# Two heads to a tile in a decode-attention kernel: 48-KB rows, one V buffer, FFN transposed, projection weights last

## The chip, the cores and the metric

The kernel runs on one core of a Trainium2 chip. The metric is the device time of one execution in microseconds (us). Several executions of one kernel agree within about 0.5% here, except single stragglers. Ratios are computed as the mean time of one kernel's fast runs over the mean of the other's fast runs in the same rounds, so they are not quite the ratio of the medians that are quoted.

Engines: DVE is the vector engine, PE the tensor engine (matmuls), ACT the scalar engine, SP the engine that here only issues DMA transfers (copies between HBM, where the inputs lie, and SBUF, the on-chip memory whose 128 partitions hold the tiles), in the order of the program. PV is short for the matmuls of the probabilities with V.

## The reference, cut to what matters

One decode step for four batches: layernorm, then attention over the last 2,048 positions of a cache of 8,192, for 32 heads of width 192, plus a SwiGLU feed-forward net (FFN), both added to x. All in bf16.

```python
W = min(4096, max(256, Sk // 4))                  # 2048
k = k_cache[:, :, Sk - W:, :]; v = v_cache[:, :, Sk - W:, :]   # [4, 32, 2048, 192]
scores = einsum("bhqd,bhkd->bhqk", q, k) * Dh ** -0.5
o = einsum("bhqk,bhkd->bhqd", softmax(scores), v)
out = x + o.reshape(B, 1, 6144) @ wo + (silu(xn @ w1) * (xn @ w3)) @ w2
```

Each byte of K and V is used once. 4 x 32 x 2,048 x 192 elements of 2 bytes, twice, are 201 of the 223 MB that are loaded.

## The kernel before

A tile of K or V is one head, for all four batches. Partition q = 4 p + b holds 64 neighbouring positions of batch b, so a row is 64 x 192 x 2 = 24,576 bytes (24 KB). The source of the transfer is *named* as 32 x 4 rows: 32 values of p outermost, then the 4 batches.

```python
def load_k(h):
    kt = kpool.tile([P, NJ, Dh], BF16, tag="kt")          # 2 buffers; V has 3
    nc.sync.dma_start(out=kt[:].rearrange("q j d -> q (j d)"),
                      in_=k_win[:, h].rearrange("b (p j) d -> p b (j d)", p=PB))   # 32 x 4 x 12288
...
def mult(u):      # DVE: a quarter of K times q, broadcast over positions
def adder(u):     # PE: six 128x512 matmuls with the identity add up 32-wide pieces
def reduce_quarter(u)   # DVE: the last sum over 32
def pv(h, half):  # PE: probabilities times V, two positions per matmul
def ge_tr(h):     # PE: float32 matmuls that regroup o for the projection with wo
```

A head is four slots (u) of this; softmax steps of earlier heads are scheduled between them. At the end come wo for the last heads and w2, whose 24 matmuls are the last work.

Of the kernel before, what the change touches and what calls it, by code (L numbers as in the profile page):

```python
# [18 lines left out]
def kernel(  # L19
# [14 lines left out]
    KBUFS: int = 2,  # L34
    VBUFS: int = 3,
    PBUFS: int = 4,
    L: int = 10,
    FFN_HEAD: int = 6,
# [9 lines left out]
    PB = P // B  # L48
    NJ = W // PB
    GQ = 4  # L50
    JQ = NJ // GQ
    NK = Dh // DD
    SCALE = float(Dh) ** -0.5
# [5 lines left out]
    NU = H * GQ  # L59
    N0 = D // 2  # L60
    N1 = D - N0
    QC = 512
    NQ = H * Dh // QC
    assert D % P == 0 and F % QC == 0 and P % B == 0 and W % (PB * GQ) == 0
    assert JQ * DD == 512 and JQ % 2 == 0 and 2 * Dh <= 512 and 0 < N1 <= 512
    assert (H * Dh) % QC == 0 and NQ % 6 == 0 and QW % P == 0 and Dh % RPP == 0 and P == HG * CT
    assert 2 * H * Dh <= NJ * Dh and KBUFS == 2 and VBUFS == 3 and L == 10

# [3 lines left out]
    kpool = ctx.enter_context(tc.tile_pool(name="kt", bufs=KBUFS))  # L72
    vpool = ctx.enter_context(tc.tile_pool(name="vt", bufs=VBUFS))
    ppool = ctx.enter_context(tc.tile_pool(name="pr", bufs=PBUFS))
    wopool = ctx.enter_context(tc.tile_pool(name="wo", bufs=2))
    small = ctx.enter_context(tc.tile_pool(name="small", bufs=3))
# [4 lines left out]
    ps_acc = ctx.enter_context(tc.tile_pool(name="ps_acc", bufs=1, space=MemoryType.PSUM))  # L81


    k_win = A_k_cache[:, :, Sk - W:Sk, :]
    v_win = A_v_cache[:, :, Sk - W:Sk, :]
    kts, vts, prs, pss, scs, exs, zs = {}, {}, {}, {}, {}, {}, {}
    wos, o_raws, rsums, rtbs, chs, ges, oTs = {}, {}, {}, {}, {}, {}, {}

    def load_k(h):
        kt = kpool.tile([P, NJ, Dh], BF16, tag="kt")  # L90
        nc.sync.dma_start(out=kt[:].rearrange("q j d -> q (j d)"),
                          in_=k_win[:, h].rearrange("b (p j) d -> p b (j d)", p=PB))
        kts[h] = kt

    def load_v(h, pieces=1):
        vt = vpool.tile([P, NJ, Dh], BF16, tag="vt")
        src = v_win[:, h].rearrange("b (p j) d -> p b j d", p=PB)
        n = NJ // pieces
        for i in range(pieces):
            nc.sync.dma_start(out=vt[:, i * n:(i + 1) * n, :].rearrange("q j d -> q (j d)"),  # L100
                              in_=src[:, :, i * n:(i + 1) * n, :].rearrange("p b j d -> p b (j d)"))
        vts[h] = vt

    def wo_load(hg):
        wo_t = wopool.tile([P, RPP * D], BF16, tag="wo")
        nc.sync.dma_start(out=wo_t[:], in_=A_wo[hg * QW:(hg + 1) * QW, :].rearrange("(p i) n -> p (i n)", i=RPP))
        wos[hg] = wo_t

    x_sb = const.tile([B, D], BF16, name="x_sb")
    nc.sync.dma_start(out=x_sb[:], in_=A_x.rearrange("b s d -> (b s) d"))  # L110
    wq_v = A_wq.rearrange("(p kc) n -> p kc n", kc=KC)
    wq_rows = []
    for k0 in range(0, KC, 2):
        n = min(2, KC - k0)
        wt = vpool.tile([P, 2, H * Dh], BF16, tag="vt")
        nc.sync.dma_start(out=wt[:, 0:n, :].rearrange("p k n -> p (k n)"),
                          in_=wq_v[:, k0:k0 + n, :].rearrange("p k n -> p (k n)"))
        wq_rows += [wt[:, i, :] for i in range(n)]
    for h in range(KBUFS):
        load_k(h)  # L120
# [5 lines left out]
    ones_ff = const.tile([P, P], FP32, name="ones_ff")  # L126
    nc.vector.memset(ones_ff[:], 1.0)

    mask_f = const.tile([P, B], FP32, name="mask_f")
    nc.vector.tensor_reduce(out=mask_f[:], in_=idf[:].rearrange("q (p b) -> q b p", b=B), axis=AX.X, op=ALU.add)  # L130
    mask_b = const.tile([P, B], BF16, name="mask_b")
    nc.vector.tensor_copy(out=mask_b[:], in_=mask_f[:])

    sel = const.tile([P, 2 * B], FP32, name="sel")
    nc.vector.tensor_reduce(out=sel[:], in_=idf[:].rearrange("q (c k) -> q k c", k=CT)[:, 0:2 * B, :],
                            axis=AX.X, op=ALU.add)

# [6 lines left out]
    xc = ppool.tile([B, D], FP32, tag="pr")  # L144
    nc.vector.tensor_scalar_add(out=xc[:], in0=xf[:], scalar1=negmean[:, 0:1])
    sq = ppool.tile([B, D], FP32, tag="pr")
    ssq = const.tile([B, 1], FP32, name="ssq")
    nc.scalar.activation(out=sq[:], in_=xc[:], func=ACTF.Square, accum_out=ssq[:])
# [6 lines left out]
    xn = const.tile([B, D], BF16, name="xn")  # L155
    nc.vector.tensor_scalar_mul(out=xn[:], in0=xc[:], scalar1=rstd[:, 0:1])
# [5 lines left out]
    xnT = const.tile([P, KC, PB, B], BF16, name="xnT")  # L162
    nc.vector.tensor_copy(out=xnT[:], in_=xnT_ps[:].unsqueeze(2).to_broadcast([P, KC, PB, B]))


    qbc = const.tile([P, H * Dh], BF16, name="qbc")
    for c0 in range(0, NQ, 6):
        qps = [pool.tile([P, QC], FP32, tag=tag, name="qps")
               for pool, tag in ((ps_add, "ps"), (ps_add, "ps"), (ps_o, "o_ps"), (ps_o, "o_ps"), (ps_m, "mt"), (ps_t, "t"))]
        for kc in range(KC):  # L170
            for i, qp in enumerate(qps):
                nc.tensor.matmul(qp[:], lhsT=xnT[:, kc].rearrange("p a b -> p (a b)"),  # L172
                                 rhs=wq_rows[kc][:, (c0 + i) * QC:(c0 + i + 1) * QC],
                                 start=(kc == 0), stop=(kc == KC - 1))
        for i, qp in enumerate(qps):
            dst = qbc[:, (c0 + i) * QC:(c0 + i + 1) * QC]
            if i % 2:
                nc.vector.tensor_copy(out=dst, in_=qp[:])  # L178
            else:
                nc.scalar.copy(out=dst, in_=qp[:])  # L180
# [8 lines left out]
    acc0 = ps_acc.tile([B, N0], FP32, name="acc0")  # L189
    acc1 = ps_acc.tile([B, N1], FP32, name="acc1")  # L190
# [8 lines left out]
    def mult(u):  # L199
        h, g = u // GQ, u % GQ  # L200
        pr = ppool.tile([P, JQ, Dh], BF16, tag="pr")
        nc.vector.tensor_tensor(out=pr[:], in0=kts[h][:, g * JQ:(g + 1) * JQ, :],  # L202
                                in1=qbc[:, h * Dh:(h + 1) * Dh].unsqueeze(1).to_broadcast([P, JQ, Dh]),
                                op=ALU.mult)
        prs[u] = pr
        if g == GQ - 1:
            kts.pop(h)
# [9 lines left out]
    def reduce_quarter(u):  # L217
        h, g = u // GQ, u % GQ
        if g == 0:
            scs[h] = small.tile([P, NJ], FP32, tag="sc", name="sc")  # L220
        nc.vector.tensor_reduce(out=scs[h][:, g * JQ:(g + 1) * JQ], in_=pss.pop(u)[:], axis=AX.X, op=ALU.add)  # L221

    def chain_lmax(h):
        lmax = small.tile([P, 1], FP32, tag="lmax")
        nc.vector.tensor_reduce(out=lmax[:], in_=scs[h][:], axis=AX.X, op=ALU.max)
        chs[h] = [lmax]

    def chain_tr(h):
        mt = ps_m.tile([P, P + 1 + B], FP32, tag="mt")
        nc.tensor.transpose(out=mt[0:1, 0:P], in_=chs[h][0][:], identity=idf[:])  # L230
        chs[h].append(mt)

    def chain_gmax(h):
        gmax = small.tile([1, B], FP32, tag="gmax")
        nc.vector.tensor_reduce(out=gmax[:], in_=chs[h][1][0:1, 0:P].rearrange("o (p b) -> o b p", b=B),  # L235
                                axis=AX.X, op=ALU.max)
        gneg = small.tile([1, PB, B], FP32, tag="gneg")
        nc.vector.tensor_scalar_mul(out=gneg[:], in0=gmax[:].unsqueeze(1).to_broadcast([1, PB, B]), scalar1=-SCALE)
        chs[h].append(gneg)

    def chain_bc(h):
        lmax, mt, gneg = chs[h]
        nc.tensor.matmul(mt[:, P:P + 1], lhsT=gneg[:].rearrange("o p b -> o (p b)"), rhs=ones_ff[0:1, 0:1],  # L243
                         start=True, stop=True)
        negm = small.tile([P, 1], FP32, tag="negm")
        nc.scalar.copy(out=negm[:], in_=mt[:, P:P + 1])
        rsum = small.tile([P, 1], FP32, tag="rsum", bufs=4)
        ex = small.tile([P, NJ], BF16, tag="ex")
        nc.scalar.activation(out=ex[:], in_=scs.pop(h)[:], func=ACTF.Exp, bias=negm[:, 0:1], scale=SCALE,  # L249
                             accum_out=rsum[:])  # L250
        rsums[h] = rsum
        exs[h] = ex

    def chain_z(h):
        ex = exs.pop(h)
        z = small.tile([P, NJ, B], BF16, tag="z")
        nc.vector.tensor_tensor(out=z[:], in0=ex[:].unsqueeze(2).to_broadcast([P, NJ, B]),  # L257
                                in1=mask_b[:].unsqueeze(1).to_broadcast([P, NJ, B]), op=ALU.mult)
        zs[h] = z

    def pv(h, half):
        o_ps, z, vt = o_banks[h % 2], zs[h], vts[h]
        n = NJ // 4
        for jj in range(half * n, (half + 1) * n):
            c = jj % 4
            nc.tensor.matmul(o_ps[c * CT:c * CT + 2 * B, :], lhsT=z[:, 2 * jj:2 * jj + 2, :],  # L266
# [31 lines left out]
    def ge_copy(h):  # L298
        hg, hl = h // HG, h % HG
        sl = slice(hl * CT, (hl + 1) * CT)  # L300
        if hl == 0:
            oTs[hg] = small.tile([P, RPP, B], BF16, tag="oT", bufs=2, name="oT")
# [132 lines left out]
```

## Time and profile before

| | before |
|---|---|
| median, 3 runs | 533.06 us (532.88 to 534.96) |
| loaded | 223 MB, 419 GB/s over the span |
| share of the span in which the load queue is busy | 97.8% |
| DVE, PE busy | 66%, 73% |

Lines of the page of the kernel before: engine totals, then the rate of the DMA in 40 slices of 13.3 us, the packets, and the load queue (packets, MB, share of 16 engines' span).

```profile
span 533.2 us, 6724 instructions
PE 391.0 (73%) x2949; PEld 177.6 (33%) x2949; DVE 349.4 (66%) x471; ACT 48.2 (9%) x150; POOL 1.1 (0%) x8
GB/s 353 430 428 431 421 442 424 438 435 428 425 435 432 428 433 431 431 427 439 429 428 431 435 426 438 430 428 435 430 433 428 433 428 440 435 420 372 422 390 140
DMA packets 11709, 223.39 MB, mean 419 GB/s; under 512 B 1304, under 2 KB 1312, under 8 KB 2720
q1 hardware_dynamic: 11680, 222.97, 97.8%
```

The queue hardly rests, and its rate is flat for most of the span. The table of windows of the kernel before (stretch, length, busy time of PE, PEld, DVE, ACT and POOL with their instructions, share of its full clock that PE was granted, share of DMA, GB/s) says the same closer, and shows the two largest places where loads were missing: a dip at 482 to 487 us, and the end. A packet counts in the window in which it starts, so a short window can show a share above 1.

```profile
100.00:200.00 100.00, 75.11 (x576) 33.97 (x576) 66.23 (x88) 13.62 (x34) 0.00 (x0) 0.88 1.00 430
200.00:300.00 100.00, 73.05 (x581) 33.47 (x581) 69.97 (x94) 5.99 (x24) 0.00 (x0) 0.83 1.01 432
482.00:487.00 5.00, 4.89 (x31) 1.55 (x29) 3.91 (x7) 0.00 (x0) 0.00 (x0) 0.82 0.57 238
524.50:533.20 8.70, 5.82 (x31) 2.91 (x28) 0.48 (x1) 0.41 (x1) 0.00 (x0) 0.80 0.02 10
```

The waits of the kernel before (engine and line, what it waited for: us in total, times, longest) show DVE waiting for K:

```profile
DVE pr L202 <- DMA kt<-in_A_k_cache_dram: 99.2, 29, 7.9
```

So the kernel is bound by its loads; 518 of its 533 us are 223.4 MB at 431 GB/s.

### The profile page before, as it was taken

The page shows a single profiled execution, that of the slowest core. Times are in us where ns is not written, and L with a number is a line of the kernel's source. Part 1 is how long each engine was busy: PE and PEld are TensorE (multiplying, and loading weights), DVE is VectorE, ACT ScalarE, POOL GpSimd, SP SyncE. Part 2 cuts the span into 40 slices and gives each one's busy share as a digit, 9 for nine tenths or more (in the row PEclk, how much of TensorE's full clock was granted, in tenths as well). Part 3 has the DMA queues.
Part 4 walks back from the last instruction along what each step waited for, and adds up shares of the span by engine and source line. Part 5 has one row for each costly group of instructions (what it writes and reads, how often), then busy time and mean ns, then how long its engine had stood idle before and what let it go on. Part 6 is the DMA issues. An engine that isn't in the chain of part 4 may idle for free.

```text
span 533.2 us, 6724 instructions
## 1 busy us (share of the span) xinstructions
PE 391.0 (73%) x2949; PEld 177.6 (33%) x2949; DVE 349.4 (66%) x471; ACT 48.2 (9%) x150; POOL 1.1 (0%) x8
## 2 busy tenths in 40 slices
PE   2876776867686978676947688586749868587987
PEld 0322232333142433232413334233313324232544
DVE  3177775787384776776757777578657778477860
ACT  2111000000222000000000000000000000000010
POOL 0000000000000000000000000000000000000000
PEclk9879776899698797688989969689996769777998
DMA  8999999999999999999999999999999999998993
GB/s 353 430 428 431 421 442 424 438 435 428 425 435 432 428 433 431 431 427 439 429 428 431 435 426 438 430 428 435 430 433 428 433 428 440 435 420 372 422 390 140
DMA packets 11709, 223.39 MB, mean 419 GB/s; under 512 B 1304, under 2 KB 1312, under 8 KB 2720
## 3 DMA queue, kind: packets, MB, share of 16 engines
q1 hardware_dynamic: 11680, 222.97, 97.8%
q8 instruction: 23, 0.38, 0.3%
q14 instruction: 6, 0.05, 0.0%
HBM read 222.96 MB, written 0.01 MB: 418 GB/s over the span
## 4 chain that ended last, share of the span: by engine, by line
DMA 59%; DVE 22%; PE 17%; issue 1%; ACT 0%; SPq 0%
DMA kt<-in_A_k_cache_dram 56%; DVE pr L202 17%; PE ps L213 7%; PE gp L294 5%; DVE sc L221 4%; DMA wt<-in_A_wq_dram 3%; PE qps L172 2%; PE o_ps L266 1%; PE acc_239 L194 1%; PE acc_240 L195 1%; DVE oT L303 1%; DVE rtb L284 1%; DVE qbc L178 0%; ACT o_raw L272 0%; DVE o_ps L186 0%
## 5 line engine op out<-in xcount | busy, mean ns | idle before, releaser
L213 PE MATMUL ps<-pr,idb 128*128 128x512 bf16 x768 | 228.9, 445 | 119.8 <-DVE sc L221 116.3
L202 DVE TENSOR_TENSOR pr<-kt,qbc 128x3072 bf16<-128x3072 bf16 x128 | 223.9, 1750 | 100.2 <-DMA kt<-in_A_k_cache_dram 99.2
L213 PEld LDWEIGHTS <-idb 128*128 128x128 bf16 x768 | 79.5, 108 | 219.8 <-issue 166.7
L221 DVE TENSOR_REDUCE sc<-ps 128x16 f32<-128x512 f32 x128 | 87.5, 684 | 10.1 <-PE ps L213 9.1
L266 PE MATMUL o_ps<-vt,z 128*8 128x384 bf16 x1024 | 59.3, 356 | 0.0
L294 PEld LDWEIGHTS gp<-sel,o_raw 128*32 128x32 f32 x768 | 46.8, 151 | 21.3 <-issue 19.2
L272 ACT COPY o_raw<-o_ps 128x384 f32<-128x384 f32 x32 | 15.3, 479 | 405.4 <-PE o_ps L266 405.4
L294 PE MATMUL gp<-sel,o_raw 128*32 128x4 f32 x768 | 49.6, 199 | 1.1 <-ACT o_raw L272 0.6
L266 PEld LDWEIGHTS <-z 128*8 128x8 bf16 x1024 | 21.1, 89 | 41.6 <-issue 32.6
L284 DVE RECIPROCAL rtb<-mt 32x4 f32<-32x4 f32 x32 | 5.7, 179 | 32.2 <-PE gp L294 31.9
L172 PE MATMUL qps<-wt,xnT 128*128 128x512 bf16 x60 | 17.7, 463 | 4.9 <-DMA wt<-in_A_wq_dram 4.9
L178 DVE CAST qbc<-qps 128x512 bf16<-128x512 f32 x6 | 3.8, 684 | 19.4 <-PE qps L172 19.4
L257 DVE TENSOR_TENSOR z<-ex,mask_b 128x256 bf16<-128x256 bf16 x32 | 13.2, 414 | 2.4 <-ACT ex L249 2.4
L194 PE MATMUL acc_239<-wo_t,oT 128*4 128x320 bf16 x48 | 13.8, 305 | 0.3 <-DVE oT L303 0.3
L195 PE MATMUL acc_240<-wo_t,oT 128*4 128x320 bf16 x48 | 13.8, 306 | 0.0
L243 PEld LDWEIGHTS mt<-ones_ff,gneg 1*128 1x128 f32 x64 | 9.4, 182 | 10.2 <-issue 9.6
L243 PE MATMUL mt<-ones_ff,gneg 1*128 1x1 f32 x64 | 12.1, 256 | 0.0
L172 PEld LDWEIGHTS <-xnT 128*128 128x128 bf16 x60 | 6.9, 115 | 15.3 <-issue 10.2
L249 ACT ACTIVATE ex<-sc,negm 128x64 bf16<-128x64 f32 x32 | 11.1, 348 | 1.0
L326 PE MATMUL gt<-w_756,xnT 128*4 128x512 bf16 x15 | 6.9, 622 | 4.2 <-DVE oT L303 2.9
L230 PE MATMUL mt<-idf,lmax 128*1 128x128 f32 x32 | 9.2, 287 | 0.0
L235 DVE TENSOR_REDUCE gmax<-mt 1x4 f32<-1x128 f32 x32 | 8.6, 269 | 0.7 <-PE mt L230 0.7
(59 smaller groups left out, 98.4 us busy)
## 6 DMA issues: line engine op xcount, KB each, us to landing
kt<-in_A_k_cache_dram SPq DMA_DIRECT2D x32, 3072.0 KB, 20.5
vt<-in_A_v_cache_dram SPq DMA_DIRECT2D x31, 3072.0 KB, 25.7
wo_t<-in_A_wo_dram SPq DMA_DIRECT2D x8, 960.0 KB, 19.4
wt<-in_A_wq_dram SPq DMA_DIRECT2D x2, 3072.0 KB, 9.8
vt<-in_A_v_cache_dram SPq DMA_DIRECT2D x2, 1536.0 KB, 14.1
w_756<-in_B_w_dram SPq DMA_DIRECT2D x1, 1920.0 KB, 23.4
w_1001<-in_B_w_dram SPq DMA_DIRECT2D x1, 1920.0 KB
wt<-in_A_wq_dram SPq DMA_DIRECT2D x1, 1536.0 KB, 19.8
```

Source lines behind the costliest of these rows:

```text
L172: nc.tensor.matmul(qp[:], lhsT=xnT[:, kc].rearrange("p a b -> p (a b)"), rhs=wq_rows[kc][:, (c0 + i) * QC:(c0 + i + 1) * QC], start=(kc == ...
L194: nc.tensor.matmul(acc0[:], lhsT=lhsT, rhs=rhs[:, 0:N0], start=first, stop=last)
L195: nc.tensor.matmul(acc1[:], lhsT=lhsT, rhs=rhs[:, N0:D], start=first, stop=last)
L202: nc.vector.tensor_tensor(out=pr[:], in0=kts[h][:, g * JQ:(g + 1) * JQ, :], in1=qbc[:, h * Dh:(h + 1) * Dh].unsqueeze(1).to_broadcast([P, ...
L213: nc.tensor.matmul(ps[:], lhsT=idb[:], rhs=pr[:, :, kk * DD:(kk + 1) * DD], start=(kk == 0), stop=(kk == NK - 1))
L221: nc.vector.tensor_reduce(out=scs[h][:, g * JQ:(g + 1) * JQ], in_=pss.pop(u)[:], axis=AX.X, op=ALU.add)
L243: nc.tensor.matmul(mt[:, P:P + 1], lhsT=gneg[:].rearrange("o p b -> o (p b)"), rhs=ones_ff[0:1, 0:1], start=True, stop=True)
L249: nc.scalar.activation(out=ex[:], in_=scs.pop(h)[:], func=ACTF.Exp, bias=negm[:, 0:1], scale=SCALE, accum_out=rsum[:])
L257: nc.vector.tensor_tensor(out=z[:], in0=ex[:].unsqueeze(2).to_broadcast([P, NJ, B]), in1=mask_b[:].unsqueeze(1).to_broadcast([P, NJ, B]), ...
L266: nc.tensor.matmul(o_ps[c * CT:c * CT + 2 * B, :], lhsT=z[:, 2 * jj:2 * jj + 2, :], rhs=vt[:, 2 * jj:2 * jj + 2, :], start=(jj < 4), stop= ...
L272: nc.scalar.copy(out=o_raw[:].rearrange("q two d -> q (two d)"), in_=o_ps[:])
L294: nc.tensor.matmul(gp[sl, i, :], lhsT=o_raw[:, part, i:Dh:RPP], rhs=sel[:, part * B:(part + 1) * B], start=(part == 0), stop=(part == 1))
```

## The change

Its intent is larger transfers and fewer small instructions. Heads i and i+16 share a tile: partition q = 8 p + u, u = (batch, head of the pair), holds 128 positions, so rows have 48 KB and a tile 6 MB. V has one buffer; K runs one pair ahead of V; w2 and the last two wo tiles are issued after the last V. The FFN's products are made transposed. The core of the diff:

```diff
-    GQ = 4
+    U = 2 * B
+    PU = P // U                      # 16
+    NJ = W // PU                     # 128
+    GQ = 8
-    vpool = ctx.enter_context(tc.tile_pool(name="vt", bufs=VBUFS))
+    vpool = ctx.enter_context(tc.tile_pool(name="vt", bufs=1))
-    k_win = A_k_cache[:, :, Sk - W:Sk, :]
+    k_win = A_k_cache[:, :, Sk - W:Sk, :].rearrange("b (h i) s d -> i (b h) s d", h=2)
+    def load_pair(dst, win, i, j0, j1):
+        src = win[i].rearrange("u (p j) d -> p u j d", p=PU)
+        nc.sync.dma_start(out=dst[:, j0:j1, :].rearrange("q j d -> q (j d)"),
+                          in_=src[:, :, j0:j1, :].rearrange("p u j d -> p u (j d)"))   # 16 x 8 x 24576
... (softmax chain and masks for 8 units; regrouping in 6 matmuls a pair instead of 12 a head; FFN transposed)
+        if i >= 2:
+            add(u0 - GQ, 0, load_k, i)
+        if not final:
+            add(u0 + 1, 0, load_v, i)
+        v = ul + 7 if not final else ul + 6       # PV of pair i: slots 6 and 7 of pair i+1
+        add(v, 7, pv, i, 0, NJ // 2 if not final else VCUT[1])
...
+    add(NU, 0, load_v, NP - 1, VCUT)
+    add(NU, 0, w2_load, 0)
+    add(NU, 0, wo_load, NG - 2)
+    add(NU, 0, wo_load, NG - 1)
+    for i in range(1, 4):
+        add(NU, 0, w2_load, i)
```

## The prediction

> **What bounds the kernel now.** The DMA queue: the page gives it 97.8% of the 16 engines' span, and the table of windows a flat 430 to 432 GB/s from 100 to 400 us. DVE (66% busy) waits 99 us for K tiles. [...] 223.4 MB at 431 GB/s are 518 us. The other 15 us of the 533.2-us span: 2.1 before the first data; about 4 of dips at 482 to 487 us (a K load issued late) and 505 to 515; 8.7 after the last load (524.5 us), for the last projections and all w2 matmuls.
>
> **What the change does.**
> 1. K and V rows of 48 KB instead of 24. The trace's packet records are linear: median 291 ns for 7,680 B, 573 for 15,360, 912 for 24,576; so 8 ns plus 36.8 per 1,000 B. Estimate for 49,152 B: 1,816 ns, 433 GB/s. 256 packets fewer per engine: -2.3 us with fewer completion packets.
> 2. DVE multiplies, adders and reduces keep shape and number (128 x 1.75 us, 768 x 0.44, 128 x 0.68). The float32 regrouping matmuls fall from 768 (50 us) to 96, softmax chains from 32 to 16. Off the critical path: 0.
> 3. One V slot: V(i) can't be issued until PV(i-1) is done, and PV stands in slots 6 and 7 of pair i, behind seven multiplies of K(i). From K(i) landing: 7 x 1.67 + 6 x 0.6 + 3.5 of chain work on DVE, then adder and two PV halves: about 22.7 us, 24 with issue latency (1.5, read at 485 us). In steady state another K stands behind V(i-1), so the queue is fed until 28 us: 4 us of margin. Estimate: 2 us lost.
> 4. At the end there is no next K. V(14) follows the last K for 14.5 us, then the queue is empty until PV(14) is done. wo and w2 need not wait, but stand behind V(15) in the one in-order SP queue. Estimated gap: 10.4 us without loads.
> 5. wo and w2 last: after the last byte remain four matmuls, the cast and the output: 5 us instead of 8.7. The old dips (4 us) go.
>
> **Sum (all on the critical path).** Start 1.8 + loads 516.3 + early gaps 2 + end gap 10.4 + tail 5 = 535.5 us. The gaps (+12) eat the gains (-10).
>
> Prediction: **535.5 us**, range 528 to 544. Faster by over 2%: 0.04; within 2%: 0.83; slower: 0.13. Without any gap it would be about 523, so a 2% gain is nearly excluded.
>
> **What would show it right or wrong.** (1) K and V packets near 1,816 ns, steady rate near 433. (3) The SP queue's waits: V loads wait for PV, yet the rate holds. (4) A hole of 8 to 12 us without DMA, some 25 us before the loads end, ended by V(15)'s issue after PV(14)'s last matmul. (5) About 5 us from last byte to end, the chain of waits ending in w2's matmuls.
>
> **What would make it wrong.** If DVE or PE are slower per slot than I take (a reduce one slot after its adder waits for PE when the clock is halved), the margin of step 3 goes and every pair opens a gap: 2 us in each of 15 is +30. If 48-KB rows read HBM at another rate, 1% is 5 us.

## The result

The time doubled: median 1047.35 us (1044.82 to 1062.45, 4 runs) against 533.49 us (532.88 to 534.96, 4 runs); ratio of the fast runs 1.9608, 95% interval 1.9545 to 1.9671. The result passed the comparison with the reference, which says little here (see the experiments). One of the four runs after, 1062.45 us, is slow and is not in the ratio.

The same lines of the page, after:

```profile
span 1045.7 us, 5471 instructions
PE 368.8 (35%) x2391; PEld 159.4 (15%) x2391; DVE 358.0 (34%) x428; ACT 26.9 (3%) x78; POOL 1.1 (0%) x8
GB/s 361 211 209 207 209 209 219 209 207 213 239 216 209 202 248 211 219 211 209 211 211 215 209 215 211 207 216 217 211 209 211 211 209 214 209 214 211 120 180 213
DMA packets 7240, 223.32 MB, mean 214 GB/s; under 512 B 808, under 2 KB 816, under 8 KB 2352
q1 hardware_dynamic: 7208, 222.96, 98.0%
```

DVE and PE did about as much work as before (358 and 369 us; 349 and 391 before). The queue is as busy as it was, 98.0%, and moves half as much. That combination is worth a pause: the share of a DMA queue counts packets in flight, not bytes, so a queue that is "98% busy" can be at half rate. Windows and waits of the kernel after:

```profile
400.00:500.00 100.00, 34.68 (x206) 14.17 (x209) 41.87 (x47) 1.73 (x7) 0.00 (x0) 0.69 1.00 212
990.00:998.00 8.00, 7.47 (x76) 2.87 (x75) 0.69 (x1) 0.42 (x1) 0.00 (x0) 0.72 0.00 0
```

```profile
DVE pr L224 <- DMA kt<-in_A_k_cache_dram: 363.4, 16, 26.7
PE o_ps L287 <- DMA vt<-in_A_v_cache_dram: 198.7, 16, 17.5
SPq L91 <- DMA vt<-in_A_v_cache_dram: 795.3, 15, 58.5
```

DVE and PE wait for K and V. The last line is the SP queue waiting for the V tile that lies in the only V buffer; it is no cause of the half rate, as the queue of loads was full all the while (share 0.99 to 1.01 in each 100 us from 100 to 900 us).

The trace also records each packet. Medians in ns, by packet size (count in brackets; not a view of the page):

```
bytes     before         after
 7,680    291 (1152)     467 (1024)     wo, w2
12,288    460  (384)     728  (256)     last wq row; of the last V before also the halves, after the last quarter
15,360    573  (256)     584  (256)     w1, w3
24,576    912 (8320)     912  (256)     K, V and wq before; wq after
49,152      -           3779 (3968)     K and V after   (estimate in the prediction: 1,816)
```

Three things stand in this table. The 48-KB packets take 2.08 times the estimate. The small packets have grown too, but only those that ran beside K or V: the first wo packets of each of six such episodes take some 600 ns, and only in the first episodes do they fall to about 300 on the way; the last two wo tiles, which run after the last V, take 291 to 308 throughout (wo is now named 64 x 2; the kernel before took 291). And the last quarter of the last V comes in packets of 12,288 bytes, which took up to 974 ns, as slow per byte as the 48-KB ones. This points away from the size of a packet; what else it is, the experiments have to show.

### The profile page after: what moved, and what is told of

Read it like the earlier page. It is cut to its first block, busy times and chain, and to the rows that moved or that the text cites. A ratio compares the mean times of both kernels' runs of the same rounds, so it can differ in the third digit from the quotient of the medians.

```text
span 1045.7 us, 5471 instructions
## 1 busy us (share of the span) xinstructions
PE 368.8 (35%) x2391; PEld 159.4 (15%) x2391; DVE 358.0 (34%) x428; ACT 26.9 (3%) x78; POOL 1.1 (0%) x8
## 4 chain that ended last, share of the span: by engine, by line
another core or an unknown queue 51%; PE 20%; DVE 18%; DMA 9%; ACT 1%; issue 0%; SPq 0%; DVEq 0%
DVE pr L224 11%; PE ps L235 11%; DMA vt<-in_A_v_cache_dram 8%; PE o_ps L287 6%; DVE sc L243 3%; DVE z L279 1%; PE qps L194 1%; DMA wq_a<-in_A_wq_dram 1%; PE f_ps L356 1%; DVE o L301 1%; ACT o_odd L293 1%; DVE o_odd L298 1%; PE acc L216 1%; PE acc L217 1%
## 5 line engine op out<-in xcount | busy, mean ns | idle before, releaser
L287 PE MATMUL o_ps<-vt,z 128*16 128x384 bf16 x1024 | 68.1, 427 | 198.7 <-DMA vt<-in_A_v_cache_dram 198.7
L287 PEld LDWEIGHTS <-z 128*16 128x16 bf16 x1024 | 29.5, 107 | 236.2 <-issue 230.4
L279 DVE TENSOR_TENSOR z<-ex,mask_b 128x1024 bf16<-128x1024 bf16 x16 | 19.3, 1209 | 1.2 <-ACT ex L271 1.2
L356 PE MATMUL f_ps<-xnT,w 128*128 128x4 bf16 x120 | 7.8, 199 | 24.4 <-DMA w<-in_B_w_dram 24.4
L325 PE MATMUL gp<-sel,o 128*64 128x4 f32 x192 | 14.6, 205 | 4.9 <-DVE o L301 4.9
L216 PE MATMUL acc<-wo_t,oT 128*4 128x320 bf16 x48 | 15.8, 342 | 0.0
L217 PE MATMUL acc<-wo_t,oT 128*4 128x320 bf16 x48 | 15.5, 339 | 0.0
L325 PEld LDWEIGHTS gp<-sel,o 128*64 128x64 f32 x192 | 13.5, 148 | 12.1 <-PE ps L235 8.7
L194 PE MATMUL qps<-wq_a,xq 128*128 128x384 bf16 x64 | 12.7, 364 | 2.2 <-DMA wq_a<-in_A_wq_dram 2.2
L194 PEld LDWEIGHTS <-xq 128*128 128x128 bf16 x80 | 8.4, 105 | 8.7 <-issue 2.9
L301 DVE TENSOR_TENSOR o<-o_odd,hp 128x384 f32<-128x384 f32 x16 | 8.9, 558 | 0.5
```

The source lines that it names most:

```text
L194: nc.tensor.matmul(qp[:], lhsT=xq[:, h2, kc].rearrange("p a b h -> p (a b h)"), rhs=row[:, h2, c * QC:(c + 1) * QC], start=(kc == 0 and h2 ...
L216: nc.tensor.matmul(acc0[:], lhsT=lhsT, rhs=rhs[:, 0:N0], start=first, stop=last)
L217: nc.tensor.matmul(acc1[:], lhsT=lhsT, rhs=rhs[:, N0:D], start=first, stop=last)
L279: nc.vector.tensor_tensor(out=z[:], in0=ex[:].unsqueeze(2).to_broadcast([P, NJ, U]), in1=mask_b[:].unsqueeze(1).to_broadcast([P, NJ, U]), ...
L287: nc.tensor.matmul(o_ps[c * CT:c * CT + 2 * U, :], lhsT=z[:, 2 * jj:2 * jj + 2, :], rhs=vt[:, 2 * jj:2 * jj + 2, :], start=(jj < 4), stop= ...
L301: nc.vector.tensor_tensor(out=o2[:], in0=o_raw[:].rearrange("q (m r) -> q r m", r=RPP).unsqueeze(3).to_broadcast([P, RPP, CT, 2]), in1=hp[ ...
```

## The experiments

Theories at the start: *size* (a 48-KB row costs more per byte), *addresses* (the rows read together lie at offsets that coincide modulo a power of two), *far heads* (two heads of a batch in one transfer; they are 16 heads of 3 MiB, so 48 MiB, apart, and the 192 MiB in the expectation of e2 is a slip). No view shows which rows are read at one moment. Kernels that move other bytes than the reference asks are wrong. The comparison with the reference passed for all of them, so it is not sharp enough to see which rows of K and V were used. The diffs are cut to the core. A list of pairs of numbers there is an access pattern: step in elements and count of each dimension, from the outermost in; where the kernel has `rearrange`, its line is written here in the same form, so that the two can be compared.

### e1: 48-KB rows as two transfers of 24 KB

```diff
-        load_pair(kts[i], k_win, i, 0, NJ)
+        for j0 in (0, NJ // 2):
+            load_pair(kts[i], k_win, i, j0, j0 + NJ // 2)
```

(V alike.)

> The changed kernel, each row of 48 KB fetched as two transfers of 24 KB (first halves of all rows, then second halves); every byte still lands where it did. Size theory (a row of 48 KB costs twice as much per byte): back to 24-KB packets near 912 ns, about 431 GB/s, 525 to 540 us. Address theory (the rows that the 16 engines read at one moment start at offsets that coincide modulo some power of two, as their pitch of 48 KB and the pairs of heads stay): packets near 1,900 ns, about 213 GB/s, 1,030 to 1,050 us.

Measured: 1031.41 us (before on that chip: 533.07). The 8,320 packets of 24,576 bytes took a median of 1,832 ns, where the same size took 912 before. The size theory has fallen.

### e2: two blocks of 24 KB at a pitch of 24 KB

```diff
+        n = NJ // 2
+        base = (i * Sk + Sk - W + (j0 // n) * PU * n + j0 % n) * Dh
+        src = bass.AP(cache.tensor, base, [[n * Dh, PU], [16 * Sk * Dh, U], [1, (j1 - j0) * Dh]])
```

> As the run before, but a partition takes two blocks of 24 KB that lie 16 blocks apart, so that rows fetched together have a pitch of 24 KB, not 48; K and V are permuted alike, the result stays right. Size theory: the same as the run before. Address theory: if offsets coincide modulo 128 KB, [...] the packets take near 912 ns, 525 to 540 us; if they coincide modulo 64 KB [...] it stays near 1,030 us. Theory of two far heads at once (engines read two heads, 192 MiB apart, at the same moment, and that alone is slow): slow in both runs, near 1,030 us.

Measured: 1014.25 us, 1,828 ns. The pitch does not matter, at least not this one.

### e3: units skewed against each other by 6 KB

```diff
-   [[NJ * Dh, PU], [16 * Sk * Dh, U], [1, n]]
+   [[NJ * Dh, PU], [(16 * Sk - 16) * Dh, U], [1, n]]
```

> The changed kernel with its 48-KB rows and one transfer a tile, but the rows of unit u (batch and head) start 6 KB x u earlier in its head[...]; the result is wrong on purpose (rows shifted by up to 112 positions). Size theory: stays near 1,045 us, packets 3,780 ns. Far-heads theory: the same. Address theory: packets near 1,816 ns, about 433 GB/s, 530 to 540 us, with the gap of 8 to 12 us near the end that was predicted.

Measured: 1054.46 us, 3,768 ns. Separating the offsets of the units did nothing. This is weaker than it was meant to be: no view shows which rows are in flight together, so the skew may have separated little.

### e4: the kernel before with rows 96 KB apart

```diff
-   in_=k_win[:, h].rearrange("b (p j) d -> p b (j d)", p=PB)          # pitch 24 KB
+   bass.AP(cache.tensor, ..., [[256 * Dh, PB], [H * Sk * Dh, B], [1, n * Dh]])   # pitch 96 KB
```

> The kernel before with its rows of 24 KB, one head per tile, but every row taken from 96 KB after the last one instead of 24 KB (the rows then span the whole head of 3 MiB); the result is wrong on purpose. Size and far-heads theories: unchanged, 912 ns a packet, about 533 us. Address theory: [...] the packets take about 1,850 ns (or 3,700) and the kernel about 1,000 us (or 2,000).

Measured: 534.95 us, 912 ns, 431 GB/s from 100 to 400 us. With e2 this ends the address theory in the form given; e14, below, is slow with the very addresses of a fast run.

What all slow kernels share is the shape in which the transfer is named: 16 x 8 rows. That suggested a fourth theory, the *naming theory*: the naming, and not the rows, decides what a packet takes. The figures of the naming theory come first, then those of the rivals.

One thing in the traces goes with it. The 808 packets under 512 B of the kernel after are all of 4 bytes: 16 for each of its 50 loads of 128 rows, and 4 each for x and for the output, which have 4 rows (the prediction calls them completion packets). Its packet records have 16 packets in flight for 927 of the 1,046 us (the kernel before: 456 of 533). I read a transfer's number of 4-byte packets as the number of engines that work on it; no view names the engine of a packet.

### e5: 48-KB rows named 32 x 4

```diff
-   [[NJ * Dh, 16], [16 * Sk * Dh, 8], [1, n]]
+   [[NJ * Dh, 32], [H * Sk * Dh, 4], [1, n]]
```

The source rows are now of one head and four batches (wrong), so they change with the naming; tile, row size, number of transfers and everything else as in the changed kernel.

> The changed kernel with its 48-KB rows, one transfer a tile, but the source named as 32 rows x 4 batches of one head instead of 16 rows x 8 units (the result is wrong on purpose). [...] packets near 1,816 ns, 433 GB/s, 528 to 540 us, with the gap of about 10 us near the end of the loads that was predicted. Size theory, already doubtful: 3,780 ns, 1,045 us.

Measured: 543.39 us (before: 534.33), 3 us more than expected. Packets of 49,152 bytes: 1,819 ns. Windows of e5:

```profile
300.00:400.00 100.00, 59.11 (x415) 24.98 (x415) 68.41 (x80) 3.23 (x12) 0.00 (x0) 0.82 1.00 432
497.00:498.00 1.00, 0.00 (x0) 0.00 (x0) 1.00 (x2) 0.00 (x0) 0.00 (x0) 1.00 0.23 98
500.00:509.00 9.00, 7.60 (x86) 3.22 (x84) 8.69 (x8) 0.00 (x0) 0.00 (x0) 1.00 0.01 5
510.00:511.00 1.00, 0.68 (x4) 0.10 (x1) 0.28 (x1) 0.00 (x0) 0.00 (x0) 1.00 1.85 516
```

With the naming changed (and the rows with it), the half rate is gone, and the hole that the prediction had put near the end stands by itself: hardly a load starts from 499 to 510 us while DVE and PE are busy. The end of it in the timeline of e5 (start, duration, engine, line): the last PV matmuls of pair 14 end at 507.80 + 1.48, and V(15), then w2, are issued.

```profile
487.81 1.76 DVE L224 TENSOR_TENSOR pr<-kt,qbc 128x3072 bf16<-128x3072 bf16 x1 [5.56 <-DMA kt<-in_A_k_cache_dram]
507.80 1.48 PE L287 MATMUL o_ps<-vt,z 128*16 128x384 bf16 x32
510.55 0.60 SPq L372 DMA_DIRECT2D w<-in_B_w_dram  x1
```

From the last K's landing (487.81) to the end of PV (509.28) are 21.5 us; the prediction had 22.7.

### e6: near rows, 24 KB, named 16 x 8

```diff
-   [[64 * Dh, 32], [H * Sk * Dh, 4], [1, n * Dh]]
+   [[9 * 64 * Dh, 16], [64 * Dh, 8], [1, n * Dh]]     # the kernel before, all rows in 3.4 MB
```

> The kernel before, 24-KB rows, but each tile named as 16 x 8 rows, all 128 out of one stretch of 3.4 MB, instead of 32 x 4 out of four batches (wrong on purpose). [...] packets near 1,830 ns, 215 GB/s, about 1,000 to 1,040 us, though no far heads are read. Far-heads theory: 912 ns, about 533 us.

Measured: 1010.39 us, 1,833 ns. This is the kernel before, made slow by the naming. Its rows are other ones too, but other rows under the old naming (e4, e7) are not slow. Its page:

```profile
PE 426.8 (42%) x2949; PEld 183.9 (18%) x2949; DVE 349.9 (35%) x471; ACT 48.2 (5%) x150; POOL 1.1 (0%) x8
GB/s 358 215 214 212 228 215 215 215 212 263 213 244 216 211 224 215 216 216 215 218 218 219 219 217 221 217 218 218 215 218 218 219 219 211 222 225 229 238 228 130
q1 hardware_dynamic: 11680, 222.97, 98.8%
```

### e7: far rows, 24 KB, named 32 x 4

```diff
+   [[4 * Sk * Dh, 32], [64 * Dh, 4], [1, n * Dh]]     # 32 heads, 12 MiB apart, in one transfer
```

> The kernel before, 24-KB rows, each tile named as 32 x 4 as before, but the 32 are 32 different heads 12 MiB apart[...] (wrong on purpose). [...] 912 ns, 431 GB/s, about 533 us. Far-heads theory: packets near 1,830 ns or more, over 1,000 us.

Measured: 545.46 us (before: 534.33), 912 ns median. Far heads are not the cause. The 2% are from one look; its rate was 383 to 425 GB/s in the first quarter of the slices and normal later, and I did not follow that up.

### e8: named 8 x 16

```diff
-   src = win[i].rearrange("u (p j) d -> p u j d", p=PU)
+   src = win[i].rearrange("u (p j) d -> u p j d", p=PU)
```

> The changed kernel with the source of a tile named as 8 units x 16 rows, so the outermost count is 8 (wrong on purpose). If the outermost count sets the number of engines, each K or V tile runs on 8. [...] packets near 3,700 ns, about 108 GB/s, about 2,000 us. Engine count [...]: packets near 1,816 ns, 217 GB/s, about 1,030 us. If neither holds and only the far heads matter: anything near the time after.

Measured: 1834.7 us; packets 3,544 ns; 116 GB/s in the window 100 to 400 us. Two lines of its page:

```profile
DMA packets 6976, 223.32 MB, mean 122 GB/s; under 512 B 544, under 2 KB 552, under 8 KB 2088
q1 hardware_dynamic: 6944, 222.96, 52.2%
```

The page after counts 808 packets under 512 B, this one 544: 264 fewer, which is 33 K and V transfers times 8. So these transfers have 8 of the 4-byte packets instead of 16, by the reading above 8 engines instead of 16, and the queue's share fell to about half (52.2%). On top of that, a packet still took about twice 1,819 ns. The median is 3,722 ns from 40 to 200 us and falls to 3,355 from 1,400 to 1,700 us.

### e11: the changed kernel with V issued from ACT

```diff
-        load_pair(vts[i], v_win, i, j0, j1)                    # nc.sync
+        load_pair(vts[i], v_win, i, j0, j1, nc.scalar)         # issued in slot 7, after PV of i-1
```

> The changed kernel as it is (16 x 8 naming, 48-KB rows, right result), but the V tiles are issued from the ACT queue, K from SP, so that K and V tiles are in flight together[...]. [...] clearly faster than 1,047 us, 600 to 950 us[...]. If an engine is simply slow[...]: 1,030 us or more, less at most the 10-us hole near the end.

Measured: 1058.88 us; packets 3,774 (SP's queue) and 3,692 ns (ACT's). For the whole run the first expectation (600 to 950 us) was wrong: by the packet records K and V were in flight together for some 480 us, and for most of that no faster (211 GB/s and 3,774 ns from 400 to 500 us). One stretch was faster: from 200 to 240 us, with both in flight, it moved 283 GB/s, and its 48-KB packets took a median of 2,694 ns. In the kernel after, no 20 us in the run of K and V have a median below 3,688. Why the gain came there and not elsewhere is open. Whether the engines hinder one another or an engine is slow by itself, this run does not tell. The next three runs were made to tell these apart, with fewer engines at work, and with the rows of e5 under other namings.

### e12, e13, e14: two engines, quarters, halves

All from e5, with 48-KB rows (wrong). e13 and e14 load the very bytes of e5 into the same places.

```diff
 e12  -   [[NJ * Dh, 32], [H * Sk * Dh, 4], [1, n]]
      +   [[H * Sk * Dh, 2], [NJ * Dh, 64], [1, n]]             # one transfer, 2 x 64
 e13  +   for r in range(4): dst[32*r:32*r+32] <- [[NJ * Dh, 8], [H * Sk * Dh, 4], [1, n]]
 e14  +   for r in range(2): dst[64*r:64*r+64] <- [[NJ * Dh, 16], [H * Sk * Dh, 4], [1, n]]
```

> The changed kernel, 48-KB rows, a tile named as 2 batches x 64 rows (wrong on purpose), so it should run on two engines[...]. [...] a packet takes 1,816 ns as on a normal load, and the two engines move 54 GB/s: about 3,800 us. [...] packets near 3,780 ns, about 7,700 us. Share of the 16 engines that is busy: about an eighth in both.

> The kernel with the source named 32 x 4 (the bytes, rows and places of that run), but each tile loaded as four transfers of 32 partitions, named 8 x 4, so each runs on 8 engines[...]. [...] packets near 1,816 ns, half of the engines busy, 217 GB/s, 1,010 to 1,050 us. [...] about 1,500 us. [...]

> As the run with quarters, but two transfers of 64 partitions, named 16 x 4, so 16 engines[...]. [...] packets near 3,700 ns, 215 GB/s, about 1,030 us. [...] packets near 1,816 ns, 433 GB/s, about 543 us.

Measured: e12 3825.89 us, e13 1028.7 us, e14 1042.95 us. The packets and the load queue of e12, of e13 and of e14:

```profile
DMA packets 6778, 223.32 MB, mean 58 GB/s; under 512 B 346, under 2 KB 354, under 8 KB 1890
q1 hardware_dynamic: 6746, 222.96, 14.0%
```

```profile
DMA packets 7769, 223.33 MB, mean 217 GB/s; under 512 B 1336, under 2 KB 1344, under 8 KB 2880
q1 hardware_dynamic: 7736, 222.96, 53.0%
```

```profile
DMA packets 7769, 223.33 MB, mean 215 GB/s; under 512 B 1336, under 2 KB 1344, under 8 KB 2880
q1 hardware_dynamic: 7736, 222.96, 98.0%
```

The 4-byte packets give the engines here too, by the reading above: leaving out 33 x 16 for K and V, 280 of the 808 of the kernel after remain, and 280 + 33 x 2 = 346 (e12), 280 + 132 x 8 = 1,336 (e13), 280 + 66 x 16 = 1,336 (e14).

e13 and e14 have nearly the same time and rate (217 and 215 GB/s), for opposite reasons: e13 has a share of 53.0% and packets of 1,819 ns, half of the engines at full speed; e14 has a share of 98.0% and packets of 3,775 ns, all engines at half speed. Only the packet time, or rate and share read together, tells them apart. All namings side by side; the engines are the 4-byte packets of one K or V transfer, share and rate are those of the window 100 to 400 us:

```
run      named    partitions   engines   DMA share   GB/s   48-KB packet, ns
                  a transfer                                (or 24-KB packet)
e5       32 x 4      128          16        1.00      427    1,819
after    16 x 8      128          16        1.00      216    3,779
e6       16 x 8      128          16        1.00      222   (1,833; before 912)
e8        8 x 16     128           8        0.53      116    3,544
e12       2 x 64     128           2        0.13       57    1,819
e13       8 x 4       32           8        0.55      220    1,819
e14      16 x 4       64          16        1.00      218    3,775
```

The packet takes 1,819 ns with 32 x 4, with 8 x 4 over 32 partitions and with 2 x 64, and about double with 16 x 8, 8 x 16 and 16 x 4 over 64. Neither the outermost count alone decides (8 is fast in e13 and slow in e8), nor the rows of one outermost item (four are fast in e5 and e13 and slow in e14; 64 are fast in e12). The figures of the naming theory for e5 to e8 and e12 to e14 came true, to within 5% of the packet time in each; those of its rivals in e8 (1,816 ns), e12 (3,780 ns), e13 (about 1,500 us) and e14 (1,816 ns) did not. The cleanest pair is e5 and e14: the same bytes, row size and places, and the packet takes twice as long with 16 x 4 in two transfers. What is shown is the dependence on the naming and the packet times. Why these namings are slow is not shown: no view of the profile names the engine of a packet or where in SBUF it writes. Three things stay open: that cause, why e8 is a little faster than double (3,544) and grows faster along the run, and why e11 was faster for 40 us.

### e9: e5 with w2 and wo ahead of the last V

```diff
-    add(NU, 0, load_v, NP - 1, VCUT)
-    add(NU, 0, w2_load, 0)          # then wo, wo, w2 1..3
+    for i in range(4): add(NU, 0, w2_load, i)
+    add(NU, 0, wo_load, NG - 2); add(NU, 0, wo_load, NG - 1)
+    add(NU, 0, load_v, NP - 1, VCUT)
     (their matmuls move ahead of the last PV, except those of the last wo tile)
```

> The 32 x 4 naming of the run with outermost count 32 (wrong on purpose), and w2 and the last two wo tiles issued ahead of the last V instead of behind it, their matmuls ahead of the last PV. If the 11-us hole there (498 to 510 us, no loads while the SP queue waits for PV of the pair before the last) is the in-order queue and nothing else, the 9 us of w2 and wo go into the hole and the time falls from 543 by 5 to 9 us, to 534 to 538; the last PV's own chain (about 5 us) then follows the last byte and takes a part back. If the hole is something else (the loads would be slow there anyhow), it stays within 2 us of 543.

Measured: median 539.93 us (4 runs) against 533.72 (11 runs of before), ratio 1.0129 (1.0103 to 1.0154). So it gained about 3.5 us on e5's single look (on another chip), less than the 5 to 9 expected. The loads did end 10 us sooner (windows of e9):

```profile
500.00:505.00 5.00, 4.80 (x36) 1.92 (x39) 4.49 (x5) 0.00 (x0) 0.00 (x0) 0.73 1.02 410
526.00:528.00 2.00, 1.87 (x43) 0.96 (x34) 0.00 (x0) 0.00 (x0) 0.00 (x0) 1.00 0.04 18
530.00:537.80 7.80, 4.62 (x24) 2.54 (x24) 0.67 (x2) 0.41 (x1) 0.00 (x0) 0.50 0.01 3
```

The hole is mostly filled, and the last bytes are there at 526 us instead of 536. Then follow 12 us without loads instead of 5: the last V's chain of PV, regrouping and projection has become the tail, on a PE whose granted clock was 0.50 at that time. So the order in the queue was the cause of most of the hole, but what is last in the queue also decides the tail, and in this kernel V last left the longer one.

### e10: the kernel before with half of w2 early

```diff
+    add(NU - 8, -1, w2_load, [(0, FC // 2)])
+    for i in range(6):
+        add(NU - 2 + i, 9, ffn_out, i, i + 1)
-    add(NU + 2, 1, w2_load, [(0, FC // 2), (FC // 2, FC - 2), (FC - 2, FC)])
+    add(NU + 2, 1, w2_load, [(FC // 2, FC - 2), (FC - 2, FC)])
```

> The kernel before, with the first half of w2 issued ahead of the last K load, into the dip at 482 to 487 us, and its 12 matmuls spread over six earlier slots instead of standing at the end (the result is right). If the tail after the last load is PE work that can be moved into PE's idle time, 1 to 3 us fewer, 530 to 532 against 533. If PE is on the critical path in those slots too, or the w2 load delays the last K and V, no gain or 1 us lost.

Measured: 533.55 us (6 runs) against 533.72 (11), ratio 1.0006 (0.9983 to 1.0029): no gain. I found no version that beats the kernel before. With 2,048 positions a head, rows of 48 KB give 16 rows per head and batch; a tile of 128 such rows is 16 x 8 or 8 x 16, and 32 items of four rows outermost would need more dimensions. No run tries that, so a right 48-KB tile at full rate is not shown here.

## Why the prediction was wrong, point by point

- **Step 1 failed, and with it the sum: "Estimate for 49,152 B: 1,816 ns, 433 GB/s".** Measured 3,779 ns and 210 to 221 GB/s. There are 4,096 K and V rows, 256 for each of 16 packets in flight, so (3,779 - 1,816) ns x 256 = 502 us; the prediction missed by 1047.35 - 535.5 = 512 us. The mis-sized term is this one. The straight line through packet sizes was itself right: e5's rows of 49,152 bytes took 1,819 ns. What the line left out is that all its points came from transfers named with 128 or 32 items outermost, and the change names its transfers 16 x 8. The diff shows this plainly (`p u j d` with p = 16); I read there only the size of the row. That the naming does it is shown by e5, e6 and e14; by what mechanism is not shown. The prediction's own warning ("if 48-KB rows read HBM at another rate, 1% is 5 us") looked to the rows that are read, which e4, e7 and e14 speak against, and was far too small.
- **Step 2** (work off the critical path) was right in that it did not matter: PE fell from 391 to 369 us, though DVE rose from 349 to 358. One count was off: the trace records each float32 matmul twice, so 768 go to 192, not to 96; 49.6 us of them became 14.6.
- **Step 3** (one V slot, 4 us of margin) could not be seen in the result, as the rate hid it. e5 shows it: its SP queue waits for PV 119.1 us in all (15 times), and the rate holds (432 GB/s from 300 to 400 us), with one gap (82 GB/s from 209 to 212 us) behind a PV that follows FFN matmuls at half clock (0.50 from 195 to 206 us); the window 200 to 300 us has 419 GB/s, which at 433 would be 3.2 us. I had 2 in total.
- **Step 4** (the hole near the end) was right. In e5 it is 11 us long, ended by V(15) after PV(14), as foretold; e9 shows that it was the order in the queue. In the kernel after there is a hole too (0 GB/s from 990 to 998 us), but there V(14) itself came late (990.5 us), so the run after alone would not have shown the predicted mechanism.
- **Step 5** (5 us of tail) was right: e5 has 5.3 us from the last loads at 536.2 us to the end.
- **The total**, with the naming put right, is 543.4 us in one look against 535.5 predicted, just inside the range. The hole (11 us against 10.4) and the gap of step 3 (3.2 against 2) were longer, the rate after the hole was 354 to 392 GB/s from 510 to 525 us, and the metric is 1.9 us longer than the profiled span; the rest I did not follow. So in this one look, and with other rows than the reference asks for, the change loses about 2% (534.33 before) even without the half rate.

## What to carry to other kernels

Read the shape in which a transfer is named, not only its bytes and row size: over 128 partitions, 32 items outermost ran at full rate here (427 to 431 GB/s from 100 to 400 us), 16 at half (216), 8 at about a quarter (116) and 2 at about an eighth (57). 128 and 64 items were seen only for the weights, and at full rate: 912 ns for 24,576 bytes of wq (128), 291 to 308 ns for 7,680 bytes of the last wo tiles (64 x 2). When loads are slow, read rate, busy share and packet time together: here half rate at 98% share was all engines with packets of double length (3,779 ns), half rate at 53% was half of the engines (packets of 1,819 ns). The line fitted through one kernel's packets held for the transfers of e5 (1,819 ns against 1,816) and not for the change (3,779), so take it to hold for transfers of the same kind only; before predicting with it, ask what else the change does to the transfer.
